# Weight sums in output buffers and in the last beats of the third and fourth chunk

## Chip, cores and metric

One core of a Trainium2 chip runs the whole program. The metric is the time of one execution in device microseconds (us).

## What is computed

Keys and values are averaged over groups of 8 positions, each of 8 batches x 8 heads attends with 576 queries over 72 pooled positions, and the 4608 tokens of 512 that come out go through two matrix products with a leaky ReLU between them:

```python
k_p = k.reshape(B, H, Sp, pool, D).mean(axis=3)
v_p = v.reshape(B, H, Sp, pool, D).mean(axis=3)
scores = scale * np.matmul(q, k_p.transpose(0, 1, 3, 2))
scores = scores - np.max(scores, axis=-1, keepdims=True)
attn = np.exp(scores)
attn = attn / (np.sum(attn, axis=-1, keepdims=True) + 1e-09)
attn_out = np.matmul(attn, v_p)
x = np.ascontiguousarray(attn_out.transpose(0, 2, 1, 3)).reshape(B * S, H * D)
h = x @ w_in
out = np.maximum(0.01 * h, h) @ w_out
```

(w_in is 512 x 2048, w_out 2048 x 512.)

## The kernel before

**Products.** Every fp32 matrix is held as a high and a low part in a faster format, and a product is three matrix products: high x high, low x high, high x low. The 4608 tokens are worked in nine chunks of 512. A chunk is a run n; the first two chunks are split over the runs 0 to 4, the third chunk is run 5, the fourth is run 6, and so on (L1120). A run has 16 slices f of the hidden layer. Per slice `m1` (L1131) makes the hidden tile ph on PE; ACT applies the leaky ReLU in place (L1148) and casts it to gh (L1151), and DVE subtracts to get gl (L1152). Two slices later `m2` (L1156) multiplies gh and gl by w_out into four accumulators acc (L1354 to L1356). `m1` and `m2` yield twice each per slice: 64 beats per run. At the end of a run the accumulators are copied to output tiles o (ACT half of each, L1393, DVE the other, L1394) and sent by SP.

**Attention beside it.** During a run, the units of the attention for the next chunk are handed out over the beats, in an order fixed before; all are done by beat 60. For the third chunk and later ones a unit's path is: scores pss on PE, exponentials e on ACT (L610), weights `at` on POOL, `rows` written to DRAM (L661) and read back as `blocks` (L670), both by SP; DVE turns a block into pp (L681, in `turn_via`), ACT casts it to pT_hi (L703), DVE makes pT_lo (L706) and masks the third row group of pT_hi (L710), and PE makes the products pa (L725 to L728) from pT and the pooled values. pa is copied to the next chunk's x as a high part xh (L744) and a low part xl (L745). The pooled values of a batch are made ahead: SP loads raw keys and values (k0raw, k1raw, L288; vremraw, eight issues of L318), POOL pools them (L265, L272), and for the leftover positions ACT makes v_parts from vremsum (L522) and DVE finishes (L524 to L531).

**The sums.** From the seventh chunk on, pairs of hidden slices are multiplied with fewer products, from sums of weight halves that the kernel forms once and keeps in DRAM (`kept`). `prepare(j, places)` (L1172) forms one pair's set: four results, each with a high part (`high`, a cast on ACT, L1186) and a low part (`low`, a subtraction on DVE, L1190), with eight sums on DVE (`do`, L1183) in x_tail as scratch; then SP sends the eight parts to `kept` (L1217), 128 KB each, and for four pairs one more half of a weight (L1220). It yields seven steps. `free(n, i)` (L1223) says in whose buffers the parts lie meanwhile: in runs 5 to 7 the upper halves of the next chunk's x buffers (which stay unused until that x is made), in run 8 buffers of the pool `one`.

**What sets the order.** `PLAN` (L1509) gives for a run how many sets are formed and in which beats; a step is issued behind the last cast and the last subtraction of that time. A scheduler then orders each engine's instructions. PE's order is the same in both versions. Pool `five` (L87, tag "o") has three buffers and is shared by pp and the output tiles.

```python
five = ctx.enter_context(tc.tile_pool(name="outs", bufs=3))
pp = five.tile([P, 3, P], F32, tag="o", name=f"pp{b}_{t}_{g}")
PLAN = {REST + 1: (2, 10, 36), REST + 2: (3, 3, 34), REST + 3: (1, 3, 20), REST + 4: (2, 3, 34)}
```

REST is 4, so the keys are the runs 5, 6, 7 and 8, and a value is (sets, first beat, last beat).

Of the kernel before, what the change touches and what calls it, by code (L numbers as in the profile page):

```python
# [24 lines left out]
def tile_pooled_attention_ffn(  # L25
# [1146 lines left out]
    def prepare(j, places):  # L1172
# [10 lines left out]
            nc.vector.tensor_tensor(out, a, b, op=op)  # L1183

        def high(i, of):
            nc.scalar.copy(places[i][0], of)  # L1186

        def low(i, of):
            h, l = places[i]
            nc.vector.tensor_tensor(l, of, h.bitcast(F32), op=SUB)  # L1190

        do(u, a21[0], a21[1], ADD)
        do(w, u, a22[0], ADD)
# [18 lines left out]
        low(2, w)  # L1212
        yield
        low(3, u)
        for i, parts_of in enumerate(places):
            for k, part in enumerate(parts_of):
                nc.sync.dma_start(kept[j, :, i, k, :], part.bitcast(F32))  # L1217
        if j < OPEN:
            with tc.issue_after(sent[-1].ins):
                nc.sync.dma_start(kept[j, :, 4], ws[0, f1].bitcast(F32)[:, :, HALF:])  # L1220
# [2 lines left out]
    def free(n, i):  # L1223

        if n < REST + FAST - 2:
            return [(h[:, HALF:], l[:, HALF:]) for h, l in zip(*x_parts(runs[n][0] + 1))]
        side, part = (runs[n][0] + 2) % 2, "hl"[i % 2]
        x = [one.tile([P, CH], F32R, tag=f"x{part}{side}_{kk}", name=f"place{i}_{kk}") for kk in range(NK)]
        return [(y[:, :HALF], y[:, HALF:]) for y in x]
# [276 lines left out]
    for b, n in loads_at.items():  # L1506
        early[max(n, REST) - 1].append(b)

    PLAN = {REST + 1: (2, 10, 36), REST + 2: (3, 3, 34), REST + 3: (1, 3, 20), REST + 4: (2, 3, 34)}  # L1509
    STEPS_OF = 7  # L1510
    left = list(range(len(PAIRS)))

    def sums_in(n):
        for i in range(PLAN[n][0]):
            yield from prepare(left.pop(0), free(n, i))

    at = 0
    for n, (c, fs, ts) in enumerate(runs[: REST + FAST - 1]):
# [11 lines left out]

                us.insert(3 * len(us) // 4, fetch)
        beats, done, beat = (2 + len(ts) // 2) * len(fs), 0, 0
        forming, formed = (sums_in(n), 0) if n in PLAN else (None, 0)
        many, begin, until = PLAN.get(n, (0, 0, 1))
        behind = 10 if final else 4
        for f in fs:
            if n == 0:
# [22 lines left out]
            for slot in slots:  # L1560
                for _ in slot:
                    beat += 1
                    while done < min(len(us), len(us) * beat // (beats - behind)):
                        us[done]()
                        done += 1
                    while forming and formed < min(1, (beat - begin) / (until - begin)) * STEPS_OF * many:
                        formed += 1
                        with tc.issue_after(casts[-1].ins), tc.issue_after(lows[-1].ins):
                            next(forming, None)
            at += 1  # L1570
        while done < len(us):
            us[done]()
# [80 lines left out]
```

## Time and profile before

| | |
|---|---|
| median of 3 runs | 919.36 us (918.85 to 920.59) |
| the profiled execution, its own time | 919.74 us |
| span of its trace | 917.9 us |
| mean granted clock of TensorE (1 is full speed) | 0.993 |
| busy: PE, DVE, ACT, POOL | 886.1, 516.0, 446.5, 221.4 us |
| third chunk (run 5), first ph product to the next run's | 253.7 to 352.0 us |
| fourth chunk (run 6) | 352.0 to 447.9 us |

PE is TensorE's matrix products, PEld its weight loads, DVE VectorE, ACT ScalarE, POOL GpSimd, SP SyncE, the queue that issues nearly all transfers. A time inside the span is counted from the span's start. A wait is put down to the releaser that came last. The profiled execution took 0.38 us more than the median of the runs.

### The profile page before, as it was taken

To read this page: it belongs to the slowest core of one execution; us is meant where nothing else is said; L and a number is where in the kernel's file an instruction comes from. 1 tells how busy PE (TensorE), PEld (TensorE's weight loads), DVE (VectorE), ACT (ScalarE), POOL (GpSimd) and SP (SyncE) were. 2 spreads that over 40 slices of the span, in tenths; PEclk is the share of its full clock that TensorE was granted. 3 is DMA by queue.
4 is the path that set the end of the run, shared out by engine and by line. 5 is a ranking of instruction groups with operands and counts; after the bars stand their busy time and mean duration, and the time that the engine had idled before them with its cause. 6 is when DMAs were issued, how large, how long until landed. Compare 5 with 4: busy or idle time off the path is not lost.

```text
span 917.9 us, 14149 instructions
## 1 busy us (share of the span) xinstructions
PE 886.1 (97%) x4731; PEld 763.0 (83%) x4731; DVE 516.0 (56%) x1229; ACT 446.5 (49%) x1397; POOL 221.4 (24%) x394
## 2 busy tenths in 40 slices
PE   5599999999999999999999999999999999999998
PEld 4478889788887888888888888888899899999997
DVE  6999569546376655764455437554664652442222
ACT  5788569435244534443444435453654554453322
POOL 4511110342525231512132132413320230010000
PEclk9889999999999999999999999999999999999999
DMA  9965231328357442734244417630784254425332
GB/s 263 314 198 177 61 78 47 83 62 201 97 164 174 113 90 75 210 97 112 54 135 113 107 27 202 169 89 1 205 210 129 72 161 123 139 78 161 104 113 71
DMA packets 157464, 116.53 MB, mean 127 GB/s; under 512 B 100688, under 2 KB 136016, under 8 KB 157392
## 3 DMA queue, kind: packets, MB, share of 16 engines
q1 hardware_dynamic: 145488, 90.86, 36.7%
q10 hardware_dynamic: 11904, 24.78, 9.0%
q8 instruction: 37, 0.61, 0.3%
q14 instruction: 35, 0.29, 0.1%
HBM read 85.07 MB, written 30.54 MB: 126 GB/s over the span
## 4 chain that ended last, share of the span: by engine, by line
PE 82%; DVE 7%; DMA 4%; ACT 3%; POOL 1%; issue 1%; SPq 1%; ACTq 0%; POOLq 0%; DVEq 0%
PE acc L1354 13%; PE acc L1356 12%; PE acc L1355 12%; PE ph L1143 8%; PE ph L1145 8%; PE ph L1144 8%; PE ends_y L1261 7%; PE ends_x L1261 5%; PE pss L600 3%; PE pa L726 1%; DMA kremraw<-in_k_dram 1%; ACT e L610 1%; PE pa L728 1%; PE pa L727 1%; DMA blocks<-rows 1%
## 5 line engine op out<-in xcount | busy, mean ns | idle before, releaser
L1354 PE MATMUL acc<-w,gh 128*128 128x512 f32 x576 | 228.3, 396 | 0.6 <-DVE o L1394 0.6
L1355 PE MATMUL acc<-w,gh 128*128 128x512 f32 x576 | 225.4, 391 | 0.0
L1356 PE MATMUL acc<-w,gl 128*128 128x512 f32 x576 | 224.9, 390 | 0.3 <-DVE gl L1292 0.3
L1143 PE MATMUL ph<-xh,w 128*128 128x512 f32 (+1 forms) x416 | 159.3, 383 | 0.3 <-DVE gl L1152 0.3
L1145 PE MATMUL ph<-xh,w 128*128 128x512 f32 (+1 forms) x416 | 156.1, 375 | 0.0
L1144 PE MATMUL ph<-xl,w 128*128 128x512 f32 (+1 forms) x416 | 156.0, 375 | 0.0
L1356 PEld LDWEIGHTS acc<-w,gl 128*128 128x128 f32 x576 | 108.2, 188 | 24.5 <-DVE gl L1292 0.8
L1354 PEld LDWEIGHTS acc<-w,gh 128*128 128x128 f32 x576 | 108.5, 188 | 19.8 <-issue 1.0
L1355 PEld LDWEIGHTS acc<-w,gh 128*128 128x128 f32 x576 | 108.5, 188 | 18.1
L610 ACT ACTIVATE e<-pss,red 128x72 f32<-128x72 f32 (+1 forms) x320 | 97.6, 329 | 37.8 <-DVE red L608 37.7
L1148 ACT ACTIVATE ph<-ph 128x512 f32<-128x512 f32 (+1 forms) x104 | 57.7, 555 | 93.7 <-PE ph L1145 92.9
L1152 DVE TENSOR_TENSOR gl<-ph,gh 128x512 fp32r<-128x512 f32 (+1 forms) x104 | 66.7, 642 | 57.8 <-ACT gh L1151 57.1
L644 POOL TENSOR_TENSOR at<-e,red 128x128 f32<-128x128 f32 (+1 forms) x120 | 50.6, 441 | 181.2 <-DVE red L641 83.7
L1145 PEld LDWEIGHTS ph<-xh,w 128*128 128x128 f32 x416 | 78.7, 189 | 14.2
L1143 PEld LDWEIGHTS ph<-xh,w 128*128 128x128 f32 x416 | 78.9, 190 | 14.0 <-DVE gl L1152 0.7
L1144 PEld LDWEIGHTS ph<-xl,w 128*128 128x128 f32 x416 | 78.9, 190 | 13.0
L610 ACT ACTIVATION_READ_ACCUMULATOR e<-pss,red 128x1 f32 (+1 forms) x320 | 68.8, 215 | 0.0
L681 DVE STREAM_TRANSPOSE pp<-blocks 128x384 f32<-128x384 f32 (+1 forms) x60 | 44.4, 759 | 42.5 <-DMA blocks<-rows 42.1
L703 ACT CAST pT_hi<-pp 128x384 fp32r<-128x384 f32 (+1 forms) x80 | 36.8, 479 | 57.8 <-DVE pp L681 54.2
L608 DVE TENSOR_REDUCE red<-pss 128x4 f32<-128x288 f32 (+1 forms) x80 | 35.8, 453 | 50.7 <-PE pss L600 49.5
L1151 ACT CAST gh<-ph 128x512 fp32r<-128x512 f32 (+1 forms) x104 | 57.8, 555 | 2.6
L600 PE MATMUL pss<-kT,qT 128*128 128x144 f32 x320 | 48.9, 294 | 4.0 <-DVE xl L745 2.1
(290 smaller groups left out, 1481.9 us busy)
## 6 DMA issues: line engine op xcount, KB each, us to landing
seat<-kept ACTq DMA_DIRECT2D x31, 512.0 KB
rows<-at SPq DMA_DIRECT2D x48, 192.0 KB
blocks<-rows SPq DMA_DIRECT2D x48, 192.0 KB
out_dram<-o SPq DMA_DIRECT2D x34, 256.0 KB
w_bits<-in_moe_w_in_dram SPq DMA_DIRECT2D x16, 512.0 KB
w_bits<-in_moe_w_out_dram SPq DMA_DIRECT2D x16, 512.0 KB
q<-in_q_dram SPq DMA_DIRECT2D x96, 64.0 KB
w<-kept ACTq DMA_DIRECT2D x21, 256.0 KB
```

The source lines that it names most:

```text
L600: nc.tensor.matmul(sc[:, 2 * SP * i : 2 * SP * (i + 1)], qT[:, p, :], kT[:, p, :, :].rearrange("d i s -> d (i s)"), start=True, stop=True,)
L610: ins = nc.scalar.activation(e[:n, h, :], scv[:n, h, :], AF.Exp, bias=mx[:n, h : h + 1], accum_out=sm[:n, h : h + 1],)
L1143: nc.tensor.matmul(ph, w[:, 0, ks], xh[kk][:, r], start=kk == 0, stop=False)
L1144: nc.tensor.matmul(ph, w[:, 0, ks], xl[kk][:, r], start=False, stop=False)
L1145: nc.tensor.matmul(ph, w[:, 1, ks], xh[kk][:, r], start=False, stop=kk == NK - 1)
L1148: nc.scalar.activation(ph, ph, AF.Prelu, alpha=0.01)
L1151: casts.append(nc.scalar.copy(gh, ph))
L1152: lows.append(nc.vector.tensor_tensor(gl, ph, gh.bitcast(F32), op=ALU.subtract))
L1261: nc.tensor.matmul(out, w[:, stay, ks], move, start=start and i + n == 0, stop=i + n == 3, skip_group_check=True,)
L1354: nc.tensor.matmul(a, gh[:, r], hi, start=first, stop=False)
L1355: nc.tensor.matmul(a, gh[:, r], lo, start=False, stop=False)
L1356: nc.tensor.matmul(a, gl[:, r], hi, start=False, stop=last)
```

## The change

The steps of `prepare` for the two sets of run 5 move from beats 10 to 36 to beats 51 to 63, and those for the three sets of run 6 from beats 3 to 34 to beats 46 to 63. In these two runs the parts no longer lie in x's buffers: `high` takes a tile from the pool `five` (tag "o") for each of the four results. In all runs the two transfers of a result to `kept` are issued right after its `low`, not all eight at the end of the set. Runs 7 and 8 keep their beats and their places.

```diff
--- before.py
+++ after.py
@@ -1183,11 +1183,16 @@
             nc.vector.tensor_tensor(out, a, b, op=op)
 
         def high(i, of):
+            if places[i] is None:
+                o = five.tile([P, 2, HALF], F32R, tag="o", name=f"place{j}_{i}")
+                places[i] = o[:, 0], o[:, 1]
             nc.scalar.copy(places[i][0], of)
 
         def low(i, of):
             h, l = places[i]
             nc.vector.tensor_tensor(l, of, h.bitcast(F32), op=SUB)
+            for k, part in enumerate(places[i]):
+                nc.sync.dma_start(kept[j, :, i, k, :], part.bitcast(F32))
 
         do(u, a21[0], a21[1], ADD)
         do(w, u, a22[0], ADD)
@@ -1212,9 +1217,6 @@
         low(2, w)
         yield
         low(3, u)
-        for i, parts_of in enumerate(places):
-            for k, part in enumerate(parts_of):
-                nc.sync.dma_start(kept[j, :, i, k, :], part.bitcast(F32))
         if j < OPEN:
             with tc.issue_after(sent[-1].ins):
                 nc.sync.dma_start(kept[j, :, 4], ws[0, f1].bitcast(F32)[:, :, HALF:])
@@ -1506,13 +1508,13 @@
     for b, n in loads_at.items():
         early[max(n, REST) - 1].append(b)
 
-    PLAN = {REST + 1: (2, 10, 36), REST + 2: (3, 3, 34), REST + 3: (1, 3, 20), REST + 4: (2, 3, 34)}
+    PLAN = {REST + 1: [(2, 51, 63, False)], REST + 2: [(3, 46, 63, False)], REST + 3: [(1, 3, 20, True)], REST + 4: [(2, 3, 34, True)]}
     STEPS_OF = 7
     left = list(range(len(PAIRS)))
 
-    def sums_in(n):
-        for i in range(PLAN[n][0]):
-            yield from prepare(left.pop(0), free(n, i))
+    def sums_in(n, which):
+        for i in range(which[0]):
+            yield from prepare(left.pop(0), free(n, i) if which[3] else [None] * 4)
 
     at = 0
     for n, (c, fs, ts) in enumerate(runs[: REST + FAST - 1]):
@@ -1530,8 +1532,7 @@
 
                 us.insert(3 * len(us) // 4, fetch)
         beats, done, beat = (2 + len(ts) // 2) * len(fs), 0, 0
-        forming, formed = (sums_in(n), 0) if n in PLAN else (None, 0)
-        many, begin, until = PLAN.get(n, (0, 0, 1))
+        forming = [[which, sums_in(n, which), 0] for which in PLAN.get(n, ())]
         behind = 10 if final else 4
         for f in fs:
             if n == 0:
@@ -1563,10 +1564,12 @@
                     while done < min(len(us), len(us) * beat // (beats - behind)):
                         us[done]()
                         done += 1
-                    while forming and formed < min(1, (beat - begin) / (until - begin)) * STEPS_OF * many:
-                        formed += 1
-                        with tc.issue_after(casts[-1].ins), tc.issue_after(lows[-1].ins):
-                            next(forming, None)
+                    for turns in forming:
+                        many, begin, until, _ = turns[0]
+                        while turns[2] < min(1, (beat - begin) / (until - begin)) * STEPS_OF * many:
+                            turns[2] += 1
+                            with tc.issue_after(casts[-1].ins), tc.issue_after(lows[-1].ins):
+                                next(turns[1], None)
             at += 1
         while done < len(us):
             us[done]()
```

The instructions of the changed kernel carry its own line numbers: the cast L1189 and the subtraction L1193 are L1186 and L1190 of before, the issue L1195 is L1217.

The change moves instructions. ACT in run 6, where the attention of the next batch starts (pp_1_0 is the second block turned, v_parts the pooled leftovers of a later batch), before and with the change:

```order
L744 CAST xh_3_3812<-pa_1_3_4452 128x256
L703 CAST pT_hi<-pp_0_0_4538 128x3x128
L703 CAST pT_hi<-pp_1_0_4551 128x3x128
L1148 ACTIVATE ph_11_4480<-ph_11_4480 128x512
L1151 CAST gh_11_4494<-ph_11_4480 128x512
L1148 ACTIVATE ph_12_4518<-ph_12_4518 128x512
L1151 CAST gh_12_4532<-ph_12_4518 128x512
L522 ACTIVATE v_parts<-vremsum_4260 128x128
L1148 ACTIVATE ph_13_4562<-ph_13_4562 128x512
```

```order
L703 CAST pT_hi<-pp_0_0_4485 128x3x128
L1148 ACTIVATE ph_12_4461<-ph_12_4461 128x512
L1151 CAST gh_12_4479<-ph_12_4461 128x512
L522 ACTIVATE v_parts<-vremsum_4195 128x128
L1189 CAST place_2_4491<-x_tail 128x256
L703 CAST pT_hi<-pp_1_0_4502 128x3x128
L1189 CAST place_3_4508<-x_tail 128x256
L1148 ACTIVATE ph_13_4525<-ph_13_4525 128x512
```

Before, the casts of both blocks stood ahead of ph_11, and v_parts behind gh_12; now v_parts and the cast of place_2 stand between gh_12 and the cast of pp_1_0.

DVE in run 5, at the last blocks of the next chunk's attention (pp_0_1, pp_1_1, pp_2_1 are turned blocks, gl_12 and gl_13 subtractions of the hidden tiles), before:

```order
L681 STREAM_TRANSPOSE pp_0_1_3653<-blocks_0_1_3651 128x4x96
L681 STREAM_TRANSPOSE pp_1_1_3673<-blocks_1_1_3671 128x4x96
L681 STREAM_TRANSPOSE pp_2_1_3691<-blocks_2_1_3689 128x2x3x32
L1152 TENSOR_TENSOR gl_12_3584<-ph_12_3562,gh_12_3583 128x512
L745 TENSOR_TENSOR xl_0_2961<-pa_0_0_3631,xh_0_2957 128x320
L1152 TENSOR_TENSOR gl_13_3628<-ph_13_3613,gh_13_3627 128x512
L745 TENSOR_TENSOR xl_1_2962<-pa_0_1_3638,xh_1_2958 128x320
L706 TENSOR_TENSOR pT_lo<-pp_0_1_3653,pT_hi 128x2x128
L710 SCALAR_TENSOR_TENSOR pT_hi<-pp_0_1_3653,marks,pT_hi 128x128
L706 TENSOR_TENSOR pT_lo<-pp_1_1_3673,pT_hi 128x2x128
L710 SCALAR_TENSOR_TENSOR pT_hi<-pp_1_1_3673,marks,pT_hi 128x128
L706 TENSOR_TENSOR pT_lo<-pp_2_1_3691,pT_hi 128x2x64
```

With the change, in two pieces:

```order
L1152 TENSOR_TENSOR gl_12_3532<-ph_12_3510,gh_12_3531 128x512
L1183 TENSOR_TENSOR x_tail<-w_0_336 128x256
L1183 TENSOR_TENSOR x_tail<-x_tail,w_0_336 128x256 x2
L1183 TENSOR_TENSOR x_tail<-w_4_657,x_tail 128x256
L1183 TENSOR_TENSOR x_tail<-x_tail,w_4_657 128x256
L1193 TENSOR_TENSOR place_1_3564<-x_tail,place_1_3564 128x256
L681 STREAM_TRANSPOSE pp_0_1_3617<-blocks_0_1_3615 128x4x96
L745 TENSOR_TENSOR xl_0_3177<-pa_0_0_3591,xh_0_3173 128x320
L1152 TENSOR_TENSOR gl_13_3588<-ph_13_3567,gh_13_3587 128x512
L1183 TENSOR_TENSOR x_tail<-x_tail,w_4_657 128x256
L1193 TENSOR_TENSOR place_0_3575<-x_tail,place_0_3575 128x256
```

```order
L745 TENSOR_TENSOR xl_1_3178<-pa_0_1_3598,xh_1_3174 128x320
L706 TENSOR_TENSOR pT_lo<-pp_0_1_3617,pT_hi 128x2x128
L710 SCALAR_TENSOR_TENSOR pT_hi<-pp_0_1_3617,marks,pT_hi 128x128
L1183 TENSOR_TENSOR x_tail<-x_tail,w_4_657 128x256
L1183 TENSOR_TENSOR x_tail<-w_4_657,x_tail 128x256
L1193 TENSOR_TENSOR place_2_3623<-x_tail,place_2_3623 128x256
L1183 TENSOR_TENSOR x_tail<-x_tail,w_4_657 128x256
L681 STREAM_TRANSPOSE pp_1_1_3647<-blocks_1_1_3645 128x4x96
L1193 TENSOR_TENSOR place_3_3633<-x_tail,place_3_3633 128x256
L681 STREAM_TRANSPOSE pp_2_1_3669<-blocks_2_1_3667 128x2x3x32
L706 TENSOR_TENSOR pT_lo<-pp_1_1_3647,pT_hi 128x2x128
L710 SCALAR_TENSOR_TENSOR pT_hi<-pp_1_1_3647,marks,pT_hi 128x128
```

Before, the three transposes stood in a row ahead of gl_12; now gl_12 and the sums of the first set stand ahead of pp_0_1, and the subtractions of place_2 and place_3 ahead of pp_2_1.

SP in run 6, at the loads of the leftovers (vremraw) and of keys (k0raw, k1raw), before and with the change:

```order
L661 DMA rows_1_1_4510<-at_1_1_4506 128x4x96
L670 DMA blocks_1_0_4549<-rows_1_0_4425 128x384
L670 DMA blocks_0_1_4606<-rows_0_1_4307 128x384
L670 DMA blocks_1_1_4620<-rows_1_1_4510 128x384
L318 DMA vremraw_4273<-in_v_dram 32x1x512 x8
L288 DMA k0raw_5178<-in_k_dram 64x2x512 x2
L288 DMA k1raw_5184<-in_k_dram 64x2x512 x2
```

```order
L661 DMA rows_1_1_4441<-at_1_1_4437 128x4x96
L670 DMA blocks_1_0_4500<-rows_1_0_4356 128x384
L670 DMA blocks_0_1_4587<-rows_0_1_4239 128x384
L318 DMA vremraw_4208<-in_v_dram 32x1x512 x8
L288 DMA k0raw_5198<-in_k_dram 64x2x512 x2
L1195 DMA kept<-place_1_4446 128x256 x2
L1195 DMA kept<-place_0_4456 128x256 x2
L670 DMA blocks_1_1_4607<-rows_1_1_4441 128x384
L288 DMA k1raw_5204<-in_k_dram 64x2x512 x2
L1195 DMA kept<-place_2_4491 128x256 x2
```

Before, all blocks stood ahead of the loads of vremraw; now blocks_1_1 stands behind k0raw and four issues into kept, and k1raw stands between it and the transfers of place_2.

## Rows read from the trace of the kernel before

**Rows 1.** The page, part 1: busy time of each engine

```profile
PE 886.1 (97%) x4731; PEld 763.0 (83%) x4731; DVE 516.0 (56%) x1229; ACT 446.5 (49%) x1397; POOL 221.4 (24%) x394
```

**Rows 2.** Waits of PE, 253 to 448: total us, times, longest

```profile
PE pa L726 <- DVE pT_lo L706: 1.6, 1, 1.6
PE acc L1354 <- DVE o L1394: 0.6, 1, 0.6
```

**Rows 3.** Chain of waits, 282 to 296 us: start us, us, what

```profile
283.94 3.96 DMA blocks<-rows
...
289.06 1.33 DVE x_tail L1183
...
290.93 0.54 DVE pT_lo L706
```

**Rows 4.** Timeline of SP, 274 to 290: start us, us, transfer

```profile
278.58 1.79 SPq L1217 DMA_DIRECT2D kept<-xh  x1
```

**Rows 5.** Chain of waits, 362 to 368.5 us

```profile
363.40 3.29 DMA out_dram<-o
```

**Rows 6.** Instructions on x_tail: ns least/median/most, first and last start

```profile
L1183 DVE TENSOR_TENSOR x_tail<-x_tail,w x48: 385/416/719, 274.1 to 593.8; 128x256 f32<-128x256 f32 x48
L1186 ACT CAST xh<-x_tail x24: 404/407/442, 275.3 to 468.7; 128x256 fp32r<-128x256 f32 x24
L1190 DVE TENSOR_TENSOR xl<-x_tail,xh x24: 399/418/956, 277.4 to 476.4; 128x256 fp32r<-128x256 f32 x24
```

**Rows 7.** Instructions of line L1217: ns, first and last start

```profile
L1217 SPq DMA_DIRECT2D kept<-xh x24: 319/392/1788, 277.3 to 469.5; - x24
```

**Rows 8.** Timeline of DVE, 326 to 346: start us, us, what [idle before]

```profile
333.13 2.06 DVE L681 STREAM_TRANSPOSE pp<-blocks 128x384 f32<-128x384 f32 x3 [0.29 <-DMA blocks<-rows]
335.11 0.66 DVE L1152 TENSOR_TENSOR gl<-ph,gh 128x512 fp32r<-128x512 f32 x1
335.69 0.48 DVE L745 TENSOR_TENSOR xl<-pa,xh 128x320 fp32r<-128x320 f32 x1
...
338.46 0.28 DVE L710 SCALAR_TENSOR_TENSOR pT_hi<-pp,marks,pT_hi 128x64 fp32r<-128x64 f32 x1
```

**Rows 9.** Timeline of PE, 341 to 345 us

```profile
343.10 0.31 PE L728 MATMUL pa<-pT_hi,v_rem 128*128 128x320 f32 x1
```

**Rows 10.** Timeline of PE, 428 to 432 us

```profile
429.99 0.28 PE L728 MATMUL pa<-pT_hi,v_rem 128*128 128x256 f32 x1
```

**Rows 11.** Timeline of ACT, 412 to 446 us

```profile
419.99 0.51 ACT L703 CAST pT_hi<-pp 128x384 fp32r<-128x384 f32 x1 [3.02 <-DVE pp L681]
...
433.52 0.31 ACT L522 ACTIVATE v_parts<-vremsum 128x128 fp32r<-128x128 f32 x1 [7.93 <-POOL vremsum L272]
```

**Rows 12.** Timeline of POOL, 414 to 440 us

```profile
417.38 0.64 POOL L272 TENSOR_TENSOR vsum<-v1raw 128x128 f32<-128x128 f32 x1
429.71 2.11 POOL L265 TENSOR_TENSOR vremraw<-vremraw 128x512 f32<-128x512 f32 x2 [11.70 <-DMA k0raw<-in_k_dram]
...
433.03 0.46 POOL L272 TENSOR_TENSOR vremsum<-vremraw 128x128 f32<-128x128 f32 x1
```

**Rows 13.** Timeline of SP, 416 to 419.2 us

```profile
416.45 2.56 SPq L670 DMA_DIRECT2D blocks<-rows  x2
419.11 0.69 SPq L318 DMA_DIRECT2D vremraw<-in_v_dram  x1
```

**Rows 14.** Timeline of PE, 438 to 440.5 us

```profile
439.13 0.28 PE L728 MATMUL pa<-pT_hi,v_rem 128*128 128x256 f32 x1
```

**Rows 15.** Timeline of SP, 410 to 437 us

```profile
433.51 1.55 SPq L288 DMA_DIRECT2D k1raw<-in_k_dram  x2
```

**Rows 16.** Timeline of PE, 34 to 36.5 us

```profile
35.47 0.90 PE L701 MATMUL pp<-ident,at 128*128 128x128 f32 x3 [5.17 <-POOL at L624]
```

**Rows 17.** Stretches: us, busy us of each engine, clock, DMA share

```profile
290.00:293.00 3.00, 1.35 (x8) 0.95 (x7) 3.00 (x8) 1.05 (x3) 2.90 (x7) 1.00 0.53 152
...
34.50:41.30 6.80, 4.86 (x19) 3.89 (x20) 6.74 (x16) 5.67 (x15) 3.72 (x8) 0.50 0.91 258
```

## The prediction

> **What bounds the kernel now.** The busy times come first [rows 1]: PE works 97% of the span, DVE 56%, ACT 49%. A change that leaves PE's instructions and their order as they are can win only time in which PE stands, and lose only by making it stand. The second view is therefore the waits of PE over the third and fourth chunk (253 to 448 us), where the moved work lies. It has two entries [rows 2]: 1.6 us before an attention product of L726 and 0.6 us before the first product of an output tile. These 2.2 us are all that the two chunks can give.
>
> The chain of waits tells where they come from. Before the first wait [rows 3] blocks arrive after 3.96 us, and then DVE does sums (L1183, 1.33 us) ahead of the pT_lo of 0.54 us that PE wants. SP's timeline shows why the blocks, issued at 283.94, were late [rows 4]: one issue into kept held the queue for 1.79 us at 278.58. The second wait is an output's copy whose buffer came free 3.29 us after a transfer that SP had issued late [rows 5], again between issues into kept.
>
> **What the change removes.** The five sets of sums leave beats 3 to 36, so both causes go: -2.2 us. The ends: -2.5 if a little idle time that the view puts down to no one goes too, and -1.6 if the output's wait stays. I take -2.2.
>
> **What it adds, by itself.** No arithmetic is new. Per set there are 8 sums and 4 subtractions on DVE and 4 casts on ACT, at 0.416, 0.418 and 0.407 us [rows 6]: some 5.0 us of DVE and 1.6 us of ACT, and 8 issues of 0.392 us on SP [rows 7]. All this existed before and runs beside PE. New are two things: where the steps stand, and whose buffers they use. DVE had to be free for 10 us in the last 13 beats of the third chunk and for 15 us in the last 18 of the fourth; it is. So the throughput costs nothing, and the cover is DVE's idle time beside PE. What is late next is decided by single waits. The pool "o" has three buffers, and the places now take turns in it with pp (attention blocks being turned), which DVE writes with L681. A place's buffer comes free only when its two transfers into kept have landed, so a pp or a place behind it waits for a landing. The trace of before has no kept landing that anything waits for. The nearest rows are 3.29 us for an output [rows 5] and 3.96 us for blocks [rows 3], both among other transfers. I take 2.2 us for a quiet queue, with 1.6 (half of the first) and 3.3 as ends, since a part sent to kept is 128 KB in one piece and little else is sent in these beats.
>
> **Third chunk.** Before, the last pT of the next block was ready at 338.74 (338.46 + 0.28) [rows 8], and PE wants it by L728 at 343.10 [rows 9], 4.4 us later. In the order shown for DVE the three transposes, contiguous before and 2.06 us together, are now pulled apart by the sums of the first set. With the durations of [rows 6, 8], from 333.13 where the transposes started: gl_12 0.7, five sums 2.1 and a subtraction 0.4, pp_0_1 0.7, xl 0.4, gl_13 0.7, a sum and a subtraction 0.8, xl 0.4, pT of pp_0_1 0.7, two sums and place_2's subtraction 1.2, together 8.1, so 341.2. Then place_2's second issue (0.4) and its landing (2.2) free the buffer that pp_2_1 takes: 343.8. Transpose, cast, pT_lo and L710 of 64 tokens take about 0.4 + 0.4 + 0.3 + 0.3 = 1.4: 345.2. That is 2.1 us after 343.10; casts of the sums ahead of ph's activation on ACT add some tenths, and I take **+2.4**. The ends: +0.5 (landing 1.6, DVE's steps at their least) and +4 (landing 3.3 and one more issue ahead).
>
> **Fourth chunk, first half.** PE wants the pT of pp_1_0 by L728 at 429.99 [rows 10]; before, its cast came at 419.99 [rows 11], with v_parts behind it at 433.52. The order of ACT turns this round: v_parts <- vremsum (L522) and place_2 now stand ahead of that cast. v_parts waits for POOL's vremsum, which ended at 433.49 (433.03 + 0.46) [rows 12], because POOL had waited 11.70 us for the loads of vremraw and k0raw. What stands behind v_parts on ACT, the cast, now waits too, and on DVE behind L524. Can vremsum come earlier? Its loads are issued from 419.11, behind two issues of blocks that take 2.56 us from 416.45 [rows 13]; the change moves the second of these back past the loads. They may then start when the first is issued, at about 416.8 or 2.3 us sooner, but not before POOL's vsum at 418.02 (417.38 + 0.64) [rows 12] if they reuse its raw buffer: 1.0 to 2.3 us sooner, so vremsum at 431.2 to 432.5. Behind it v_parts 0.3, then on DVE L524 0.5, place_2's subtraction 0.4, a sum 0.4, L527 0.3, pT_lo 0.4, L710 0.3 give 433.8 to 435.1, or 0.5 less with overlapping starts. Against 429.99: 3.3 to 5.1, and I take **+3.7**, toward the lower end, since PE itself comes some tenths later here (-1.6 + 2.4). The ends are +2 (loads land faster without the earlier kept traffic) and +5.
>
> **Fourth chunk, second half.** PE wants the next pT at 439.13 [rows 14], now 3.9 us later (-2.2 + 2.4 + 3.7): 443.0. SP has k1raw (1.55 us, behind vremsum [rows 15]) ahead of place_2's issues: vremsum at about 432, k1raw until 433.5, two issues until 434.3, landing 436.5. Then the next set's first place is cast and subtracted (437.4), issued and landed (440.4), and pp_0_1 and pp_1_1 follow a chain of two more buffers: place_2 of this set and its landing (443.8), pp_1_1 0.7, cast 0.5, pT_lo 0.4, L710 0.3: 445.7. That is **+2.7**, with ends 0 (landings of 1.6, three in a row) and +5.
>
> **Later parts.** The outputs at the start of the fifth and sixth run and the next chunk's first x have over 7 us, and the last set of the fourth chunk nothing that PE wants behind it. These cost nothing; if the cover went, the first output copies would wait a landing, 2 us.
>
> **Sum.** -2.2 + 2.4 + 3.7 + 2.7 = +6.6 on the profiled 919.74, or 926.3. The median of the runs shown is 0.4 lower, so the forecast is **926.0 us**. With every end at its low: -2.5 + 0.5 + 2 + 0 = 0.0; at its high: -1.6 + 4 + 5 + 5 = +12.4. The four ends do not come together, and the waits are linked: a long first wait gives the transfers behind it time.
>
> **A rule that could add to it.** Where PE stood 5.17 us, before 35.47 [rows 16], the granted clock was 0.50 (1.2 GHz) in the stretch from 34.5 to 41.3; where it stood for the first wait of [rows 2], at 290 to 293, it was 1.00 (2.4 GHz) [rows 17]. A wait of 3.7 us lies between, so it may cost a stretch at half clock. In such a stretch PE does half the work: 6.8 us of it cost 3.4 us, and half as much 1.7. The Trainium skill, "TensorE: Matmul & The Clock Gate", section "HAM oscillation — how this bites in real kernels", says that waits of this size drop the clock each time; the 0.50 after 5.17 us agrees, and the 1.00 after 1.6 us does not speak against it.
>
> **The rivals.**
> - *The covers hold, and it is faster* (the other side). The landings are quick and vremsum's loads land early, so that pT_hi of pp_1_0 is cast before 429.6 and pp_2_1 before 341.7. Then -2.2 stays: 917.2. For it: DVE is only 56% busy, and the loads' issues do come earlier. Against it: vremsum would have to be 5.5 us sooner than 433.49, against 2.3 that the issue order gives. Chance 0.10.
> - *One small wait takes the place of the two that go* (no change): one of the three new waits is short, 2 to 2.5 us, and the rest are covered: 919 to 920, at 919.4. For it: 4.4 us of slack in the third chunk. Against it: the order of ACT behind v_parts. Chance 0.14.
> - *The clock falls too*: as the forecast plus 1.7 to 3.4: 927.7 to 929.4, say 928.5. For it: the half clock after 5.17 us. Against it: part of each wait is broken up by single products of L725 and L726. Chance 0.16.
> - *The change doesn't do what it says*: excluded for the order, as DVE's, ACT's and SP's rows are moved as its words tell.
>
> **How the numbers follow.** The forecast has 0.60 (slower by 3 to 9 us), the clock's fall 0.16, no change 0.14, faster 0.10. No change is within 0.2%, 1.84 us, about what can be told apart. The forecast's own low corner lies inside that bound too, so 0.02 of it goes to no change: faster 0.10, same 0.16, slower 0.74. The range: from 918.2, leaving out faster and a tail of the low side, up to 930.5, which takes in most of the clock's case.
>
> **What would show it.** Right: the two entries [rows 2] are gone; three new waits stand on attention products at about 342, 430 and 440 us, for pT_lo or pT_hi; ACT's idle time ahead of v_parts ends with POOL's vremsum and the cast of pp_1_0 follows it; DVE's transposes wait for kept transfers. Wrong: no wait at 430 us, or vremsum near 427; or waits over 5 us, or a granted clock under 1.00 after one of them.

## The result and the profile after

The changed kernel takes 927.31 us (median of 6 runs, 926.48 to 929.35) against 920.31 us for the kernel before on the same chip (918.85 to 920.59): a ratio of 1.0079, with a 95% interval of 1.0064 to 1.0094. It is slower by 7.0 us. The forecast was 926.0 us, between 918.2 and 930.5.

The profiled execution has a span of 924.7 us, 6.8 us more than before. The busy times of the page answer to [rows 1]:

```profile
PE 889.2 (96%) x4731; PEld 764.6 (83%) x4731; DVE 515.3 (56%) x1229; ACT 447.9 (48%) x1397; POOL 218.9 (24%) x394
```

PE's busy time has risen by 3.1 us for the same 4731 products. The same product is counted longer where the granted clock is lower, so this is a first sign that the clock fell somewhere. The waits of PE from 250 to 460 us, which hold the third and fourth chunk, answer to [rows 2] (total us, times, longest):

```profile
PE pa L725 <- ACT pT_hi L703: 4.3, 3, 2.1
PE pa L726 <- DVE pT_lo L706: 0.6, 1, 0.6
PE acc L1356 <- DVE o L1396: 0.6, 1, 0.6
```

The wait of 1.6 us near 291 us is gone. The output's wait of 0.6 us is still there. The cast pT_hi is now waited for three times. PE's timeline says where, in two pieces (start us, us, what, in brackets the idle time before it and its releaser):

```profile
341.92 0.41 PE L725 MATMUL pa<-pT_hi,v_hi 128*128 128x320 f32 x1 [1.19 <-ACT pT_hi L703]
```

```profile
428.95 0.39 PE L1145 MATMUL ph<-xh,w 128*128 128x512 f32 x1
431.46 0.38 PE L725 MATMUL pa<-pT_hi,v_hi 128*128 128x256 f32 x1 [2.12 <-ACT pT_hi L703]
432.44 0.39 PE L726 MATMUL pa<-pT_lo,v_hi 128*128 128x256 f32 x1 [0.60 <-DVE pT_lo L706]
...
433.79 0.63 PE L1356 MATMUL acc<-w,gh 128*128 128x512 f32 x1
...
444.37 0.38 PE L725 MATMUL pa<-pT_hi,v_hi 128*128 128x256 f32 x1 [1.00 <-ACT pT_hi L703]
```

Three places stand out: 1.19 us at 341.92, then 2.12 and 0.60 us at 431.46 and 432.44, then 1.00 us at 444.37. And behind the second place a product of 512 columns takes 0.63 us, where the one at 428.95 took 0.39. The view of stretches (us, busy us of PE, PEld, DVE, ACT and POOL with their counts, granted clock, DMA share, GB/s) shows the clock there:

```profile
420.00:430.00 10.00, 9.34 (x42) 7.39 (x40) 7.05 (x16) 2.40 (x5) 3.39 (x4) 1.00 0.58 165
...
434.00:436.00 2.00, 2.00 (x6) 1.52 (x6) 2.00 (x5) 0.40 (x2) 0.84 (x1) 0.50 0.79 253
```

From 434 to 436 us TensorE ran at 0.50 of full speed, 1.2 GHz instead of 2.4 GHz. From 438 us on it is at 1.00 again.

PE executes the same list of products in both kernels. So the start of each product can be set against its start before, and the difference grows by what each place costs:

| stretch of PE's list | difference before it, us | after it, us | cost, us |
|---|---|---|---|
| the wait near 291 us (gone) | 0.0 | -2.07 | -2.1 |
| pa near 342 us | -2.07 | -0.46 | +1.6 |
| pa near 430 us, until L726 starts | -0.46 | +2.69 | +3.2 |
| the products behind it, until 436 us | +2.69 | +4.43 | +1.7 |
| pa near 444 us | +4.43 | +6.11 | +1.7 |
| one wait for gl near 596 us, other places | +6.11 | +6.65 | +0.5 |

The sum is 6.6 us, where the forecast had summed to +6.6. Its terms were not these, as the section on the prediction tells. The table accounts for the traced execution, the fastest of the six (926.48 us); the median is 0.8 us longer.

### The profile page after: what moved, and what is told of

The parts are those of the page before. It is cut to its first block, busy times and chain, and to the rows that moved or that the text cites. A ratio compares the mean times of both kernels' runs of the same rounds, so it can differ in the third digit from the quotient of the medians.

```text
span 924.7 us, 14152 instructions
## 1 busy us (share of the span) xinstructions
PE 889.2 (96%) x4731; PEld 764.6 (83%) x4731; DVE 515.3 (56%) x1229; ACT 447.9 (48%) x1397; POOL 218.9 (24%) x394
## 4 chain that ended last, share of the span: by engine, by line
PE 80%; DVE 6%; DMA 5%; ACT 4%; SPq 2%; issue 1%; POOL 1%; ACTq 0%; POOLq 0%; DVEq 0%
PE acc L1356 12%; PE acc L1357 12%; PE acc L1358 12%; PE ph L1143 8%; PE ph L1145 8%; PE ph L1144 8%; PE ends_y L1263 7%; PE ends_x L1263 5%; PE pss L600 3%; ACT e L610 1%; PE pa L726 1%; DMA kremraw<-in_k_dram 1%; PE pa L728 1%; DMA blocks<-rows 1%; PE pa L727 1%
```

## Where the waits come from

**Near 342 us.** The chain of waits of the changed kernel (start us, us, what) goes through a transfer of a place, and DVE's timeline shows what came behind it:

```profile
339.32 1.34 DMA kept<-place
...
341.52 0.36 ACT pT_hi L703
...
341.92 0.41 PE pa L725
```

```profile
341.10 0.38 DVE L681 STREAM_TRANSPOSE pp<-blocks 128x192 f32<-128x192 f32 x1 [0.45 <-issue]
```

The second transfer of place_2 is issued at 339.32 us, and DVE turns pp_2_1, which takes its buffer, at 341.10. The landing took under 1.8 us: the chain counts the first 1.34 of them, until DVE's own work ended, and the 0.45 of idle time behind it as "issue". Then the block is cast, and PE goes on.

**Near 430 us.** Two things end there at nearly the same time. The timelines of ACT, DVE, POOL and SP of the changed kernel, one after the other:

```profile
430.39 0.31 ACT L522 ACTIVATE v_parts<-vremsum 128x128 fp32r<-128x128 f32 x1 [5.17 <-POOL vremsum L272]
...
430.90 0.51 ACT L703 CAST pT_hi<-pp 128x384 fp32r<-128x384 f32 x1
```

```profile
428.71 0.86 DVE L681 STREAM_TRANSPOSE pp<-blocks 128x384 f32<-128x384 f32 x1 [1.97 <-DMA kept<-place]
```

```profile
426.53 2.17 POOL L265 TENSOR_TENSOR vremraw<-vremraw 128x512 f32<-128x512 f32 x2 [10.14 <-DMA vremraw<-in_v_dram]
```

```profile
416.52 5.39 SPq L318 DMA_DIRECT2D vremraw<-in_v_dram  x8
422.01 1.35 SPq L288 DMA_DIRECT2D k0raw<-in_k_dram  x2
423.46 1.98 SPq L1195 DMA_DIRECT2D kept<-place  x4
```

On ACT, v_parts waits 5.17 us for POOL's vremsum, and the cast of pp_1_0 (430.90) stands behind it. Before, that cast was made at 419.99 [rows 11]. On DVE the turning of pp_1_0 itself waits 1.97 us for a transfer of a place, until 428.71. That transfer was the second of four issued from 423.46 on, behind eight loads of vremraw and two of k0raw. It is place_1's second part, issued at 424.09, so it landed 4.5 us after its issue. So there are two candidates for one wait, the order (on ACT, and on DVE behind it) and the landing, and the experiments have to tell them apart. In this execution the order ended last, as the chain of waits shows:

```profile
429.95 0.42 POOL vremsum L272
...
430.39 0.32 ACT v_parts L522
...
430.73 0.46 DVE vremsum L524
...
432.06 0.34 DVE pT_lo L706
...
432.44 0.39 PE pa L726
```

**Near 444 us.** ACT's and DVE's timelines:

```profile
441.18 0.51 ACT L703 CAST pT_hi<-pp 128x384 fp32r<-128x384 f32 x1
...
443.81 0.51 ACT L703 CAST pT_hi<-pp 128x384 fp32r<-128x384 f32 x1 [1.33 <-DVE pp L681]
```

```profile
440.21 0.86 DVE L681 STREAM_TRANSPOSE pp<-blocks 128x384 f32<-128x384 f32 x1 [0.22 <-DMA kept<-place]
...
442.32 0.68 DVE L1152 TENSOR_TENSOR gl<-ph,gh 128x512 fp32r<-128x512 f32 x1
442.93 0.85 DVE L681 STREAM_TRANSPOSE pp<-blocks 128x384 f32<-128x384 f32 x1
```

Here a landing held DVE for 0.22 us only. The cast of the first block stands behind ph's activation on ACT, and the second block is turned behind gl on DVE: the wait comes from the orders of ACT and DVE.

## The experiments

The theory: the cost is a sum of single waits, from the order of v_parts and from landings of places in the shared output buffers, with a fall of the clock on top. Rivals: the load as such (sums and transfers squeezed into the end of a run), the shared buffers alone, or the order of v_parts alone.

Each experiment ran beside the kernel before on its own chip (medians of 919.70 to 919.80 us), and its ratio is to those runs. A trace is of one execution, and the executions of one kernel differ by up to 5 us, so the single waits of a trace need not be those of the median.

### One chunk at a time

```diff
-    PLAN = {REST + 1: [(2, 51, 63, False)], REST + 2: [(3, 46, 63, False)], REST + 3: [(1, 3, 20, True)], REST + 4: [(2, 3, 34, True)]}
+    PLAN = {REST + 1: [(2, 51, 63, False)], REST + 2: [(3, 3, 34, True)], REST + 3: [(1, 3, 20, True)], REST + 4: [(2, 3, 34, True)]}
```

> Only the third chunk's sums (run 5) are late and in output buffers; the fourth chunk's keep their old beats and x's buffers. Theory of single waits: the wait near 291 us goes (-2.0), one of 1.2 to 1.5 us stands near 342 us, none at 430 or 444 us, and the output's 0.6 us near 367 stays: 0.5 to 0.8 us under before, about 919.7. Rival of load (sums and transfers squeezed into the end of a run slow whatever runs there): two fifths of the added time, +3 us, and no single wait that accounts for it.

Measured: 920.67 us, ratio to before 1.0009 (0.9997 to 1.0021). PE's waits from 250 to 460 us:

```profile
PE pa L725 <- ACT pT_hi L703: 2.2, 1, 2.2
PE acc L1356 <- DVE o L1396: 0.6, 1, 0.6
```

The wait near 291 us went, and one of 2.2 us near 342 took its place, longer than the 1.2 to 1.5 expected. In these two chunks two sets late cost nothing but this wait, and load as a cause falls for the third chunk. (Two later waits for gl, near 590 and 667 us, are 0.7 and 0.9 us, against 0.3 each before.)

```diff
-    PLAN = {REST + 1: [(2, 51, 63, False)], REST + 2: [(3, 46, 63, False)], REST + 3: [(1, 3, 20, True)], REST + 4: [(2, 3, 34, True)]}
+    PLAN = {REST + 1: [(2, 10, 36, True)], REST + 2: [(3, 46, 63, False)], REST + 3: [(1, 3, 20, True)], REST + 4: [(2, 3, 34, True)]}
```

> Only the fourth chunk's sums (run 6) are late and in output buffers. Theory of single waits: the wait of 1.6 us near 291 stays, none at 342; the waits of 2.7 us near 430, the stretch at half clock behind it (1.7 us) and some 1.5 us near 444 are there as with the whole change: +6.5 to +8 over before, about 927.5. Rival of load: +4 (three of five sets).

Measured: 929.22 us, ratio 1.0098 (1.0081 to 1.0116), more than expected. The fourth chunk carries the whole loss. PE's waits were longer in this execution than with the whole change, and the old one near 291 us is among them:

```profile
PE pa L725 <- ACT pT_hi L703: 5.2, 2, 3.8
PE pa L726 <- DVE pT_lo L706: 1.8, 2, 1.2
```

The clock fell twice: behind the wait of 3.8 us near 432, and again behind one of 1.45 us near 445 (0.50 from 448 to 450 us). The second fall is not in the trace of the whole change. The output's wait near 367 us is gone here and stayed with the whole change, though in neither an issue into kept stands among the outputs on SP. Why is not shown.

### The buffers alone, the issues alone

```diff
-    PLAN = {REST + 1: [(2, 51, 63, False)], REST + 2: [(3, 46, 63, False)], REST + 3: [(1, 3, 20, True)], REST + 4: [(2, 3, 34, True)]}
+    PLAN = {REST + 1: [(2, 10, 36, False)], REST + 2: [(3, 3, 34, False)], REST + 3: [(1, 3, 20, True)], REST + 4: [(2, 3, 34, True)]}
```

> The places lie in the output buffers as with the change, but the sums keep the old beats (10 to 36 and 3 to 34). Theory of single waits: no wait at 342, 430 or 444; the old wait near 291 stays and may grow by a landing (0 to 2 us), the outputs near 365 wait a landing more (0 to 2 us): +0 to +3 over before, about 921.5. Rival of shared buffers alone: most of the change's +7 is there, 925 or more.

Measured: 922.37 us, ratio 1.0026 (1.0013 to 1.0038), as expected. The places in the output buffers at the old beats cost 2.4 us, a third of the change's loss: the old wait stays, and two outputs wait for landings near 366 us. The chain of waits there goes through a place:

```profile
363.32 3.90 DMA kept<-place
```

The third part of the change, each result sent right behind its subtraction, was put into the kernel before by itself (old beats, x's buffers):

```diff
-    PLAN = {REST + 1: [(2, 51, 63, False)], REST + 2: [(3, 46, 63, False)], REST + 3: [(1, 3, 20, True)], REST + 4: [(2, 3, 34, True)]}
+    PLAN = {REST + 1: [(2, 10, 36, True)], REST + 2: [(3, 3, 34, True)], REST + 3: [(1, 3, 20, True)], REST + 4: [(2, 3, 34, True)]}
```

> Before's beats and x's buffers; only the transfers of a part are issued right behind its subtraction. Theory of single waits: the waits near 291 and 367 stay within 0.7 us of before, and the waits for gl near 589 and 665 grow by 0.3 to 0.6 each as in the earlier runs: +0.3 to +1.5, about 921. Rival: the earlier issues relieve SP, and the time falls by 0.5 or more.

Measured: 919.53 us, ratio 0.9997 (0.9985 to 1.0009). Of the expected increase at the waits for gl the trace shows the one near 589 us (0.9 us against 0.3), and none near 665; the time did not rise. This part costs nothing that can be measured.

### The wait near 430 us: order or landing

First the order was put back, with the landing left as it is. `turned` holds the cast and the last step of each pp; the lines that fill it and the rest of the indented call are left out here:

```diff
-            pin(nc.scalar.mul(v_parts, rem, 1.0 / POOL))
+            with tc.issue_after(turned["cast", 4, 1, 0].ins) if b == 5 else nullcontext():
+                pin(nc.scalar.mul(v_parts, rem, 1.0 / POOL))
             yield
-            pin(nc.vector.scalar_tensor_tensor(
+            with tc.issue_after(turned["end", 4, 1, 0].ins) if b == 5 else nullcontext():
+                pin(nc.vector.scalar_tensor_tensor(
```

> The whole change, but v_parts (ACT) and the step on vremsum behind it (DVE) stand behind the cast and the pT of pp_1_0. Theory of single waits: pp_1_0 is still turned only when place_0's transfers have landed, near 428.7, but its cast and pT_lo follow at once, by 430.7: the two waits of 2.7 us near 430 shrink to 1.0 to 1.5, the granted clock stays at 1.00 (2.4 GHz) and gives back 1.7: 3.0 us under the whole change, about 924. Rival of shared buffers alone (the landing of place_0 sets the wait, v_parts would have been late anyway): within 0.5 us of the whole change.

Measured: 927.34 us, ratio 1.0078 (1.0057 to 1.0098), the same as the whole change. DVE's timeline:

```profile
427.55 0.42 DVE L1189 TENSOR_TENSOR x_tail<-w,x_tail 128x256 f32<-128x256 f32 x1
431.81 0.87 DVE L685 STREAM_TRANSPOSE pp<-blocks 128x384 f32<-128x384 f32 x1 [3.84 <-DMA kept<-place]
```

The turning of pp_1_0 waited 3.84 us, until 431.81, for the landing of a place. The chain of waits shows that transfer, again the second of four:

```profile
427.14 4.59 DMA kept<-place
```

The cast followed at 432.71 with nothing of v_parts in its way, and PE still waited 2.70 and 1.03 us. So a landing alone can make a wait of this size, and the time is the one that the rival had foretold. But it is not quite the changed kernel's landing. In this execution the loads ahead had been issued later, since a row transfer ahead of them landed later (SP waited 3.3 us for it, and 1.5 in the changed kernel): pp_1_0 was turned 1.2 us after PE had come to stand, there 0.6 us before. An estimate from the changed kernel's own rows: turned at 428.71 and cast with nothing ahead of it, pT_hi would be ready near 430.1, 0.8 us after PE came to stand at 429.34. That landing alone would have left about a third of the 2.12 us. This execution also lost 1.7 us to a fall of the clock near 342 us, which the changed kernel's trace does not have.

Then the landing was taken out, with the order left as it is. With run 6's sums from beat 49, the scheduler puts the turning of pp_1_0 ahead of all places, but v_parts stays ahead of its cast:

```diff
-    PLAN = {REST + 1: [(2, 51, 63, False)], REST + 2: [(3, 46, 63, False)], REST + 3: [(1, 3, 20, True)], REST + 4: [(2, 3, 34, True)]}
+    PLAN = {REST + 1: [(2, 51, 63, False)], REST + 2: [(3, 49, 63, False)], REST + 3: [(1, 3, 20, True)], REST + 4: [(2, 3, 34, True)]}
```

> The whole change with run 6's sums from beat 49, not 46. In the issue order pp_0_0 and pp_1_0 are now turned ahead of every place, so no landing of a place holds them; but v_parts on ACT and the step on vremsum on DVE still stand ahead of the cast and the turning of pp_1_0. If the landing of place_0 made the wait near 430: it goes, and the half clock with it, 4 us under the change, about 923. If v_parts made it: it stays at 2.5 us or more, 926 to 928. If either alone suffices (both end at about the same time): it stays, as with v_parts.

Measured: 931.70 us, ratio 1.0127 (1.0107 to 1.0148). ACT's and PE's timelines:

```profile
432.58 0.31 ACT L522 ACTIVATE v_parts<-vremsum 128x128 fp32r<-128x128 f32 x1 [6.98 <-POOL vremsum L272]
...
434.18 0.51 ACT L703 CAST pT_hi<-pp 128x384 fp32r<-128x384 f32 x1 [1.00 <-DVE pp L681]
```

```profile
434.74 0.58 PE L725 MATMUL pa<-pT_hi,v_hi 128*128 128x256 f32 x1 [4.95 <-ACT pT_hi L703]
```

No landing holds pp_1_0 now, and the wait is 4.95 us: v_parts waited 6.98 us for vremsum, DVE's step on vremsum and the turning of pp_1_0 stood behind it, and so did the cast. So the order alone is enough. The wait is longer than with the change, as three blocks stand ahead of the loads on SP again and the first load is issued at 418.46, not at 416.52. (The traced execution, of 934.12 us, is the slowest of four.) In the changed kernel the landing and vremsum came within 2 us of each other. Taking away the landing leaves the order; putting back the order leaves the landing, and then it counts how late that one is.

Both were taken away with a start at beat 51, where pp_1_0 is turned and cast ahead of the places and of v_parts:

```diff
-    PLAN = {REST + 1: [(2, 51, 63, False)], REST + 2: [(3, 46, 63, False)], REST + 3: [(1, 3, 20, True)], REST + 4: [(2, 3, 34, True)]}
+    PLAN = {REST + 1: [(2, 51, 63, False)], REST + 2: [(3, 51, 63, False)], REST + 3: [(1, 3, 20, True)], REST + 4: [(2, 3, 34, True)]}
```

> The whole change with run 6's sums from beat 51: pp_1_0 is turned and cast ahead of the places and ahead of v_parts, both as in before. All theories of the wait near 430: it goes, the granted clock stays at 1.00 there, and only 1 to 3 us near 442 (pp_0_1 and pp_1_1 among the places) stay: 922 to 924. Rival of load: as much work is now squeezed into 12 beats, not 17, so 927 or more.

Measured: 927.62 us, ratio 1.0083 (1.0069 to 1.0097). The wait near 430 us went, as expected. The total did not fall, since the next pair of blocks paid. PE's timeline, the chain of waits and the stretches show it:

```profile
444.31 0.58 PE L725 MATMUL pa<-pT_hi,v_hi 128*128 128x256 f32 x1 [5.33 <-ACT pT_hi L703]
```

```profile
436.16 3.19 DMA kept<-place
```

```profile
430.00:434.00 4.00, 4.00 (x22) 3.43 (x21) 0.37 (x1) 0.61 (x2) 3.88 (x5) 1.00 0.01 3
...
444.00:448.00 4.00, 3.31 (x11) 2.83 (x12) 3.75 (x11) 1.62 (x5) 0.00 (x0) 0.50 0.38 127
```

pp_0_1 and pp_1_1 now stood among the places: a landing of 3.19 us, then sums, then a wait of 5.33 us on PE and a clock of 0.50 behind it. The expectation of 922 to 924 missed because I had priced this wait by the changed kernel's 1.0 us. The time is also the one that the rival of load had foretold (927 or more); that it is a single wait all the same is seen in the trace, and the load is tested by itself further below.

### Another queue

Here ACT issued the places' transfers, with the order of v_parts put back by the edit shown above:

```diff
-                nc.sync.dma_start(kept[j, :, i, k, :], part.bitcast(F32))
+                queue = nc.scalar if late else nc.sync
+                queue.dma_start(kept[j, :, i, k, :], part.bitcast(F32))
```

> The whole change with v_parts behind the cast of pp_1_0 and, in runs 5 and 6, the transfers of the places issued by ACT, so that they no longer stand behind the loads of vremraw and k0raw on SP. Theory of single waits (the landing of place_0, late by SP's order, holds pp_1_0): pp_1_0 is turned 2 us or more sooner, the waits near 430 shrink from 2.7 to under 1 and the granted clock stays at 1.00, and near 444 1 us goes: 3 to 5 us under the change, about 923. Rival (the landing itself is slow, since the loads fill the 16 DMA engines, whoever issues): pp_1_0 is turned less than 1 us sooner, 926 or more.

Measured: 928.32 us, ratio 1.0092 (1.0074 to 1.0109). ACT's timeline, with the same columns:

```profile
425.04 0.41 ACT L1196 CAST place<-x_tail 128x256 fp32r<-128x256 f32 x1 [1.71 <-DMA vremraw<-in_v_dram]
...
427.06 0.58 ACT L1154 ACTIVATE ph<-ph 128x512 f32<-128x512 f32 x1 [1.61 <-DMA vremraw<-in_v_dram]
...
428.67 0.59 ACT L1157 CAST gh<-ph 128x512 fp32r<-128x512 f32 x1 [1.02 <-DMA vremraw<-in_v_dram]
```

The transfers did not get past the loads. ACT stood at three issues until a load of vremraw that SP had issued had landed, and with it ph's activation and gh's cast stood. The trace's semaphore events say why: the transfers of this stretch report their landings on eight semaphores (counters that instructions wait for), which both queues take in turn, and ACT's issue at 424.62 first waits for the semaphore of the third load of vremraw, which SP had issued at 420.83. So it is the program that ties the queues together. pp_1_0 was turned at 433.22 us, not at 428.71 as with the whole change, and since ACT stood, the run does not show how fast a transfer of a second queue would land.

### All of it behind the attention

The strongest test of load against single waits is to squeeze the sums more, but behind the last block:

```diff
-    PLAN = {REST + 1: [(2, 51, 63, False)], REST + 2: [(3, 46, 63, False)], REST + 3: [(1, 3, 20, True)], REST + 4: [(2, 3, 34, True)]}
+    PLAN = {REST + 1: [(2, 57, 63, False)], REST + 2: [(3, 57, 63, False)], REST + 3: [(1, 3, 20, True)], REST + 4: [(2, 3, 34, True)]}
```

> The whole change with both starts moved to beat 57: all five sets late, all in output buffers, even more squeezed than with the change. Theory of single waits: none of the waits at 342, 430 and 444 us; the first outputs of run 7 near 455 us may wait for landings of places (0 to 3 us); -2.0 near 291: 918 to 922, about 920, 7 under the change. Rival of load or of the shared buffers as such: 925 to 930.

Measured: 921.25 us, ratio 1.0012 (1.0002 to 1.0021). None of the three waits is left; a wait of 3.0 us has come at the outputs of the fourth chunk, whose copies wait for a place's landing. PE's waits and the chain:

```profile
PE acc L1356 <- DVE red L640: 3.0, 1, 3.0
```

```profile
457.77 1.99 DMA kept<-place
```

All five sets are late, in output buffers, in fewer beats than with the change, and the ratio to before is 1.0012 where the change has 1.0079. Load is not the cause.

### A version that is faster than both

If only waits count, the third chunk's sums may go behind its attention, and the fourth's may stay where they were. In these three kernels parts in x's buffers are again sent at the end of a set. First with the fourth chunk's sums begun a little later, so that they don't delay the outputs:

```diff
-    PLAN = {REST + 1: [(2, 51, 63, False)], REST + 2: [(3, 46, 63, False)], REST + 3: [(1, 3, 20, True)], REST + 4: [(2, 3, 34, True)]}
+    PLAN = {REST + 1: [(2, 57, 63, False)], REST + 2: [(3, 8, 36, True)], REST + 3: [(1, 3, 20, True)], REST + 4: [(2, 3, 34, True)]}
```

> Run 5's sums start at beat 57, when all blocks of the next chunk have been turned (output buffers); run 6's stay in x's buffers and start at beat 8, not 3, so that the outputs of run 5 are sent first; parts outside the output buffers are again sent at the end of a set. Theory of single waits: the wait near 291 us goes, none comes at 342, the output's wait near 367 goes or halves: 1.7 to 2.5 us under before, about 917.7. Rival of load: sums squeezed into 7 beats cost as before or more, 920 or over.

Measured: 919.20 us, ratio 0.9991 (0.9980 to 1.0003), not the 917.7 expected. In the trace, of an execution of 917.27 us near the fastest of the twelve, PE waits no more near 291, 342 and 367 us, but near 395 us it waits 2.3 us for gl:

```profile
PE ph L1143 <- DVE gl L1152: 2.3, 1, 2.3
```

In DVE's order gl_6 had come to stand behind the turning of two blocks (pp_3_1, pp_4_1), whose landing it then waited for. With beats 10 to 36 gl_6 stands ahead of them:

```diff
-    PLAN = {REST + 1: [(2, 51, 63, False)], REST + 2: [(3, 46, 63, False)], REST + 3: [(1, 3, 20, True)], REST + 4: [(2, 3, 34, True)]}
+    PLAN = {REST + 1: [(2, 57, 63, False)], REST + 2: [(3, 10, 36, True)], REST + 3: [(1, 3, 20, True)], REST + 4: [(2, 3, 34, True)]}
```

> As the run before it, with run 6's sums in beats 10 to 36: all outputs of run 5 are copied and sent ahead of the first sum, so the output's wait goes too (-0.6 to -0.9), and gl_6 stands ahead of the last two blocks: 2.5 to 3 us under before; if gl waits behind a block all the same, 1 to 2.5 us are given back.

Measured: 919.89 us, ratio 0.9998 (0.9989 to 1.0007). Another gl took the wait (gl_5, behind the turning of pp_3_0, whose block landed 5.14 us after its issue), and the clock fell. PE's waits and the stretch behind:

```profile
PE ph L1143 <- DVE gl L1152: 2.8, 1, 2.8
```

```profile
392.50:394.50 2.00, 2.00 (x7) 1.56 (x6) 2.00 (x6) 1.58 (x3) 1.08 (x2) 0.51 0.30 102
```

With the old beats for the fourth chunk:

```diff
-    PLAN = {REST + 1: [(2, 51, 63, False)], REST + 2: [(3, 46, 63, False)], REST + 3: [(1, 3, 20, True)], REST + 4: [(2, 3, 34, True)]}
+    PLAN = {REST + 1: [(2, 57, 63, False)], REST + 2: [(3, 3, 34, True)], REST + 3: [(1, 3, 20, True)], REST + 4: [(2, 3, 34, True)]}
```

> Run 5's sums from beat 57 in output buffers, run 6's as before (beats 3 to 34, x's buffers, sent at the end of a set). The wait near 291 goes (-2.0), none at 342, the output's 0.6 us near 367 stays, the wait of 2.3 us for gl near 395 of the run with beats 8 to 36 doesn't come, as gl_6 stands ahead of the last two blocks again: 1.8 to 2.2 us under before.

Measured: **917.58 us, ratio to before 0.9975 (0.9964 to 0.9985)**, faster than both kernels. A single wait is left in the two chunks:

```profile
PE ph L1143 <- DVE gl L1152: 0.6, 1, 0.6
```

The output's wait went as well, which I had not expected. SP's timeline shows it: the two outputs are issued at 359.12 and 359.73 us, ahead of the chunk's first issue into kept at 362.64, where before they went at 362.79 and 363.40, behind two of them. What turned this order round was not followed up.

## Why the prediction was right, and where not

- **The bound.** PE's order is unchanged and the cost is where PE stands: the table of differences accounts for 6.6 of the 6.8 us between the two spans.
- **What goes.** The wait near 291 us went and gave 2.1 us. The output's 0.6 us did not: its transfer went 1.5 us sooner than before, at 361.86 us, but took 4.16 us to land, so the buffer came free at 366.02, against 366.69 [rows 5], while PE came 0.5 us sooner too. The step that took "both causes" as gone failed for this one. The forecast wavered here: its sum uses -2.2, its term for the fourth chunk's first half -1.6.
- **Third chunk, +2.4.** The mechanism was right (pp_2_1 waits for place_2's landing), the size was off: issue and landing took 1.8 us, not 0.4 + 2.2, and the term measured +1.6. That is the smallest of six: in the five other kernels with this chunk's sums from beat 51 the wait was 2.0 to 2.6 us, against 1.19 here, so the term is nearer to +2.4 there.
- **Fourth chunk, first half, +3.7.** Measured +3.2. The order behind v_parts is real, as the chain of waits and the run from beat 49 show. But vremsum came at 430.35, not at 431.2 to 432.5: POOL's vsum had ended sooner (416.39), the loads started 2.6 us sooner, not 1.0 to 2.3, and took 0.6 us less until POOL could begin. And a second cause that the forecast left out here held pp_1_0 until 428.71: the landing of place_1 (the expectations call it place_0) took 4.5 us behind the loads, not the 2.2 of a quiet queue. In the changed kernel it ended 1.7 us before v_parts could start; with the order put back it was enough for a wait of 2.7 us.
- **Fourth chunk, second half, +2.7.** Measured +1.7. The step that failed here is the chain over the buffers, with three landings of 2.2 us in a row: in the changed kernel a landing held DVE for 0.22 us, and the wait came from the orders of ACT and DVE. With the start at beat 51 a landing (3.19 us) does stand in the chain of this wait.
- **The clock.** It fell behind the wait near 430 us and cost +1.7 us, the low end of the rival with a chance of 0.16. So that rival happened, and with it one of the forecast's own signs of being wrong, a granted clock under 1.00. The three waits came 2.3 us shorter than the forecast's 8.8 (6.5), and the clock with the smaller places (1.7 + 0.5) made up for 2.2. That the total was right to some tenths is luck in this part.
- **The rival on the other side** (the covers hold) needed vremsum 5.5 us sooner; it came 3.1 us sooner. And with the order put back a landing still stood in the way.

The Trainium skill, "TensorE: Matmul & The Clock Gate", section "HAM oscillation — how this bites in real kernels", says that waits of some 3 to 5 us bring the clock down each time. The granted clock of 0.50 behind 3.8 us (the fourth chunk alone), 4.95 us (start at beat 49) and 5.33 us (start at beat 51) agrees; the 1.00 behind a wait of 3.0 us (row in the last section) does not. The falls behind 2.0 us and less (last section) are shorter waits than it speaks of.

## What to carry to other kernels

Work that is moved to where an engine is idle brings its buffers and its place in each queue along: look at what stands behind each wait on an in-order engine, and at whose landing frees each buffer that the moved work shares. Where two waits end within a few us of each other, taking away one may show nothing; take away each alone and then both, and look in each trace at how late the one that is left came. Moving the third chunk's sums behind the last consumer of the shared buffers gained 0.25%; moving both chunks' sums there cost 0.12%, as the next user of the buffers waited; the change, in among the consumers, lost 0.8%.

## What was not expected of the hardware

- **The clock does not follow the length of a wait alone.** It fell to 0.50 behind waits of 2.0 us (with the order put back, near 342), 2.8 us (the third chunk's sums behind the attention, the fourth's in beats 10 to 36) and 4.95 us, and stayed at 1.00 behind waits of 2.2 us (the third chunk alone, near 342) and 3.0 us (all behind the attention, near 462). The place near 342 shows it best, as PE's list is the same in all kernels: the clock fell behind 2.0 and 2.3 us (order put back, ACT's queue) and stayed at 1.00 behind 2.1, 2.2 and 2.6 us (beat 49, third chunk alone, beat 51). The shortest with a fall is 1.45 us (fourth chunk alone, near 445). A fall cost 1.7 us near 430 in the changed kernel and some 2.7 us behind the wait of 4.95 us. What decides is not shown. Three stretches behind waits, of the third chunk alone, of the order put back and of all behind the attention:

```profile
344.00:346.00 2.00, 2.00 (x11) 1.68 (x10) 1.93 (x6) 1.05 (x3) 0.00 (x0) 1.00 0.00 0
```

```profile
344.00:346.00 2.00, 2.00 (x6) 1.57 (x5) 1.96 (x7) 0.83 (x2) 0.00 (x0) 0.50 0.05 18
```

```profile
462.00:464.00 2.00, 1.74 (x8) 1.46 (x9) 2.00 (x10) 1.44 (x7) 0.92 (x3) 1.00 0.71 131
```

- **The landing of a place's transfer**, counted from its issue, took under 1.8 us near 340 us and 3.2 to 4.6 us where other transfers were on their way (3.19 with the start at beat 51, 3.90 with the old beats, 4.5 and 4.59 behind the loads of vremraw), for the same 128 KB.
